# The last four down-projection tiles: one pair of tiles as seven products, placed between the other pair's two plain tiles

## The chip, the cores and the metric

The kernel runs on one core of one Trainium2 chip. The metric is the device time of one execution in microseconds; the median of three runs stands for a kernel. The profile is taken from one further execution. Engine names in the profile: PE is TensorE (matmul), PEld its weight load, DVE is VectorE, ACT is ScalarE, POOL is GpSimd, SP is SyncE, from which all transfers are issued here.

## The reference

```python
x = A_x                                          # 2048 tokens x 448
a, b = x_norm @ dft_hid_re.T, x_norm @ dft_hid_im.T
h  = x + dft_seq_re @ a - dft_seq_im @ b         # Fourier mixing
g, u = h_norm @ w_gate, h_norm @ w_up            # 448 -> 1792
h2 = h + (gelu(g) * u) @ w_down                  # 1792 -> 448, added to h
```

x_norm and h_norm are layer norms over the 448 columns. The change touches only the last line's product, `(gelu(g) * u) @ w_down`, called "down" here, for the last 512 of the 2048 tokens.

## The kernel before

**Products.** Every f32 operand is split into two f16 numbers, a high half (`hi_part`, line 103, on ACT) and a low half (`lo_part`, line 107 or 109, on DVE: the operand less its high half). A product of two operands is three f16 matmuls: high x high, high x low, low x high.

**Down in pairs.** The tokens are handled in pairs of tiles, p = 0 to 7, each of two 128-token tiles (g = 0, 1). The contraction of 1792 is cut into 14 slices f of 128; chunk n (0 to 6, `NC` = 7) joins slices n and n + 7. A pair's hidden values for one chunk are then a 2 x 2 matrix of blocks (g by slice), and the weights for the chunk are a 2 x 2 matrix of blocks too (slice by half of the 448 output columns, `HD` = 224). Pairs 0 to 5 multiply these 2 x 2 matrices with seven block products in place of eight: `strassen_mm` (line 651) runs 7 products x 3 terms = 21 matmuls of 128 x 224 per chunk, into four PSUM banks `a0` to `a3`. The list `STRASSEN` (line 147) names, in order, which of seven left operands meets which of seven right ones:

```python
STRASSEN = [(0, 5), (1, 4), (3, 0), (2, 1), (6, 6), (5, 3), (4, 2)]
```

Left operands 0 and 1 are blocks of the hidden values themselves; 2 to 6 are sums and differences of blocks. For pairs 0 to 5 these are made one or more chunks ahead by `dn_sums` (line 804: two POOL instructions of 256 elements a partition, one DVE add of 128) and split by `dn_split` (line 811). The right operands (`wd`, line 670) are made once, early. After its seventh chunk, a pair is drained (class `Drain`, line 603): ACT copies two banks to SBUF (`copy`), DVE adds three and then one half bank into the result `hr` (`bank2`, `bank3`, line 621), and POOL adds the copies in eight instructions (`sums`, line 649); `dn_store` (line 842) sends the 448 KB to DRAM.

**The last two pairs.** Pairs 6 and 7 hold the tokens of the last quarter (q = 3), whose hidden values come out while pairs 2 to 5 are multiplied. They are not summed: `last_hi` and `last_lo` (lines 854 and 857) split each slice f into `last["h"]` in f16 (both halves, all 14 slices, four tiles), as it is made. After the last gate/up step the four tiles (j, g), j = pair - 6, are multiplied plainly by `last_mm` (line 867): 14 slices x 3 terms x 2 column halves = 84 matmuls of 128 x 224 a tile. The diagonal weight blocks come from `wd`, the other two from `last["w"]`. `last_out` (line 886) adds a bank into `hr` on DVE and sends it off. The fourth tile is done in column halves, each with its own bank, so that only half of it is left to add and send at the end.

**What orders the work.** The scheduling is by hand: each engine runs its instructions in the order in which the code issues them, and waits in that order. A table `side` (line 904) holds pieces of side work by step t and place k; `do(t, k)` issues them. At the end of the loop over t, pair 5 is still being drained: `do(N_GU, k)` issues the last slices' high and low halves, pair 5's `bank3` and the first two of its eight POOL sums; `do(N_GU + 1, 3)` to `do(N_GU + 3, 3)` issue the other six and the store, in the code before right after the first plain tile. Buffers rotate: `hq`, `dn_s` have two each, `dn_w` three.

Of the kernel before, what the change touches and what calls it, by code (L numbers as in the profile page):

```python
# [8 lines left out]
F16 = mybir.dt.float16  # L9
F32 = mybir.dt.float32  # L10
# [3 lines left out]
P = 128  # L14
# [18 lines left out]
def kernel(  # L33
# [6 lines left out]
    w_down: bass.AP,  # L40
    out: bass.AP,
):

# [24 lines left out]
    V, A, G, PE = nc.vector, nc.scalar, nc.gpsimd, nc.tensor  # L70
# [7 lines left out]
    ps_tr = ctx.enter_context(tc.tile_pool(name="ps_tr", bufs=1, space=bass.MemoryType.PSUM))  # L78
# [23 lines left out]
    def hi_part(dst, src, scale=1.0):  # L102
        A.activation(dst, src, AF.Copy, scale=scale)  # L103

    def lo_part(dst, src, hi, scale=1.0):
        if isinstance(scale, float) and scale == 1.0:
            V.tensor_sub(dst, src, hi)  # L107
        else:
            V.scalar_tensor_tensor(dst, src, scale, hi, op0=ALU.mult, op1=ALU.subtract)  # L109
# [181 lines left out]
    class Weights:  # L291
# [8 lines left out]
        def sums(self):  # L300
            gate, up = self.raw[:, 0], self.raw[:, 1]
            s = self.s = dft.tile([P, 10, P], F32, tag="s", name=f"gu_s{self.f}")
            V.tensor_add(s[:, 0:3], up[:, 0:3], up[:, 3:6])
            V.tensor_sub(s[:, 3:6], s[:, 0:3], gate[:, 0:3])
            V.tensor_sub(s[:, 6:8], gate[:, 0:2], up[:, 0:2])
            V.tensor_sub(s[:, 8:10], gate[:, 4:6], s[:, 4:6])
# [194 lines left out]
    for k, f in enumerate(reversed(range(NF))):  # L501
        n = 17 + 3 * k
# [4 lines left out]
    for b in range(NB):  # L507
        for j in range(2):
            n = (b + 1) * NT + 1 + 6 * j
# [41 lines left out]
    for n in range(N_STEPS):  # L551
        b, c = divmod(n, NT)
# [50 lines left out]
    class Drain:  # L603
# [27 lines left out]
        def bank3(self):  # L631
            self.add(3, 6, 1.0)

        def sums(self, parts):
            x11, x12, x21, x22 = self.x
            M3, M4, M2, M5 = self.v
            ops = (
                (G.tensor_add, x12, M3),
                (G.tensor_sub, x21, M4),
                (G.tensor_add, x21, M2),  # L640
                (G.tensor_add, x12, M5),
                (G.tensor_sub, x11, M4),
                (G.tensor_add, x22, M3),
                (G.tensor_sub, x11, M5),
                (G.tensor_sub, x22, M2),
            )
            for k in parts:
                op, x, m = ops[k]
                op(x, x, m)

    def strassen_mm(acc, a_of, b_of, first, last, products):

        for n in products:
            k, m = divmod(n, 3)
            a, b = STRASSEN[k]
            la, lb = ((0, 0), (0, 1), (1, 0))[m]

            PE.matmul(  # L658
                acc[k // 2][:, k % 2 * HD : (k % 2 + 1) * HD],
                a_of(la, a),  # L660
                b_of(lb, b),
                start=first and m == 0 and k % 2 == 0,
                stop=last and m == 2,
                skip_group_check=True,
            )

    fpool = ctx.enter_context(tc.tile_pool(name="fpool", bufs=1, side="right", reuse_waits="tile"))
    ps_gu = ctx.enter_context(tc.tile_pool(name="ps_gu", bufs=1, space=bass.MemoryType.PSUM, reuse_waits="tile"))
    ps_dn = ctx.enter_context(tc.tile_pool(name="ps_dn", bufs=1, space=bass.MemoryType.PSUM, reuse_waits="tile"))
    wd = fpool.tile([P, NF // 2, 2, 7, HD], F16, name="wd")  # L670
# [29 lines left out]
    TQ = 2 * P  # L700
# [25 lines left out]
    def ftile(tag, bufs, name, n=TQ):  # L726
        return fpool.tile([P, n], F32, tag=tag, bufs=bufs, name=name)

    hh, hq = {}, {}
# [67 lines left out]
    NC = NF // 2  # L797
    dn_s, dn_w, acc_d, hr = {}, {}, {}, {}
# [5 lines left out]
    def dn_sums(d):  # L804
        t = dn_hid(d)
        s = dn_s[d] = fpool.tile([P, 5, P], F32, tag="dn_s", bufs=2, name=f"dn_s{d}")
        G.tensor_add(s[:, 0:2], t[:, 0:2], t[:, 2:4])  # L807
        G.tensor_sub(s[:, 2:4], t[:, 1:4:2], t[:, 0:4:2])
        V.tensor_add(s[:, 4], t[:, 0], t[:, 3])

    def dn_split(d):
        w = dn_w[d] = fpool.tile([P, 2, 7, P], F16, tag="dn_w", bufs=3, name=f"dn_w{d}")
        for src, dst in ((dn_hid(d)[:, 0:4:3], slice(0, 2)), (dn_s.pop(d), slice(2, 7))):
            hi_part(w[:, 0, dst], src)
            lo_part(w[:, 1, dst], src, w[:, 0, dst])
# [21 lines left out]
    def dn_drain(p):  # L837
        v = [ftile(f"v{k}", 1, f"v{k}_{p}", D) for k in range(2)]
        return Drain(hr[p], acc_d.pop(p), v, 1.0 / (H_SC * W_SC))

    def dn_store(p):
        nc.sync.dma_start(outr[p // 4, p % 4], hr[p])
# [3 lines left out]
    last = {}  # L846
# [20 lines left out]
    def last_mm(j, g, banks):  # L867

        tok = slice(g * TQ + j * P, g * TQ + (j + 1) * P)
        one = len(banks) == 1  # L870
        for cs in ((0, 1),) if one else ((0,), (1,)):
            for f in range(NF):
                k, n = divmod(f, NC)
                for m, (lh, lw) in enumerate(((0, 0), (0, 1), (1, 0))):
                    for c in cs:
                        w = wd[:, n, lw, k] if c == k else last["w"][:, lw, n, k]
                        PE.matmul(  # L877
                            banks[0][:, c * HD : (c + 1) * HD] if one else banks[c][:, 0:HD],
                            last["h"][:, lh, f, tok],
                            w,  # L880
                            start=f == 0 and m == 0 and c == cs[0],
                            stop=f == NF - 1 and m == 2,
                            skip_group_check=True,
                        )

    def last_out(j, g, ps, c, n):
        p = 6 + j
        h = hr[p][:, g, c * HD : (c + n) * HD]
        V.scalar_tensor_tensor(h, ps[:, 0 : n * HD], 1.0 / (H_SC * W_SC), h, op0=ALU.mult, op1=ALU.add)
        nc.sync.dma_start(outr[p // 4, p % 4][:, g, c * HD : (c + n) * HD], h)  # L890

    def dn_ahead(t):

        if t in (NF - 4, NF - 1):
            dn_sums(int(t == NF - 1))
        if t == NF - 2:
            dn_split(0)
        if NF <= t < 6 * NC + 12:
            dn_sums(t - 12)

    N_GU = 4 * NF
# [4 lines left out]
    def do(t, k):  # L906
        for what in side.pop((t, k), ()):
            what()
# [25 lines left out]
    for t in range(3 * NF, N_GU):  # L934
        f = t % NF
        if f < NF - 1:
            n, k = divmod(f, 2)
# [28 lines left out]
    for t in range(N_GU):  # L966
        q, f = divmod(t, NF)
# [24 lines left out]
        if q == 0:  # L992
            dn_ahead(t)
            cur.xy()
            prev = cur
            cur = GateUp(t + 1)
            cur.open()
            prev.yz()
            if d == -1:
                prev.c12_plus()  # L1000
            continue
# [3 lines left out]
        dn_mm(d, range(0, 8))  # L1005
        cur.xy()
        dn_ahead(t)
        dn_mm(d, range(8, 18))
        do(t, 1)
# [11 lines left out]
    prev.c_last()  # L1021
    for k in (1, 2, 0, 3):
        do(N_GU, k)
    banks = [(ps_tr, "tr"), (ps_gu, "X"), (ps_gu, "Y"), (ps_gu, "Z"), (ps_dn, "a0")]
    banks = [pool.tile([P, 512], F32, tag=tag, name=f"last_{tag}") for pool, tag in banks]
    for i in range(4):
        j, g = divmod(i, 2)
        last_mm(j, g, banks[i : i + 1] if i < 3 else banks[3:5])
        if i < 3:
            last_out(j, g, banks[i], 0, 2)  # L1030
        else:
            last_out(j, g, banks[3], 0, 1)
            last_out(j, g, banks[4], 1, 1)
        for t in range(N_GU + 1, N_GU + 4) if i == 0 else ():
            do(t, 3)
    assert not side


# [57 lines left out]
```

## Time and profile before

| what | us |
|---|---|
| median of 3 runs (728.07 to 730.27) | 728.22 |
| the profiled execution, its own time | 729.39 |
| its span, first to last instruction | 727.6 |
| TensorE busy | 719.5 |
| VectorE busy | 500.1 |
| ScalarE busy | 271.5 |
| GpSimd busy | 234.3 |
| the four plain tiles, first matmul to last tile's end | 692.1 to 724.5 |
| first plain tile starts / second / third | 692.1 / 700.2 / 708.2 |

The span is what the profile can see; the execution's time holds a further 1.8 us around it. A line of the profile names the source line, the engine, the instruction, the tiles written and read, its shape, and the count. In a timeline the first two numbers are the start and the duration in us, and a bracket gives the idle time before the instruction and what ended it. In a table of windows each engine has its busy time in the window and its count of instructions. In a group of instructions the numbers behind the bar are the busy time in us and the mean duration of one in ns.

### The profile page before, as it was taken

What the parts mean: (1) busy time and instruction counts of PE and PEld (TensorE: products, weight loads), DVE (VectorE), ACT (ScalarE), POOL (GpSimd) and SP (SyncE); (2) the same over time, 40 slices, a digit from 0 to 9 for tenths busy, and PEclk for the clock granted to TensorE, in tenths of its full rate; (3) what the DMA queues carried; (4) which work ended last, traced back from release to release, by engine and by line L of the source; (5) the groups of instructions that cost most, each with busy time, mean ns of one, the idle gap of its engine ahead of it and who ended that gap; (6) DMA issues with size and microseconds to landing.
All of it is one profiled execution on the core that took longest, in us unless ns stands there. A gap on an engine that the chain in (4) does not pass through costs nothing.

```text
span 727.6 us, 13421 instructions
## 1 busy us (share of the span) xinstructions
PE 719.5 (99%) x5330; PEld 499.2 (69%) x5330; DVE 500.1 (69%) x1026; ACT 271.5 (37%) x535; POOL 234.3 (32%) x274
## 2 busy tenths in 40 slices
PE   8999999999999999999999999999999999999998
PEld 5444444444444444444488889999999999999998
DVE  6888657486665866440477778788787877989730
ACT  4444704156133452221144443443444433454410
POOL 0000000000000001000057865577676766858430
PEclk9999999999999999999999999999999999999999
DMA  8766566577657976621057754757538496556411
GB/s 278 227 223 223 176 224 202 183 215 271 232 195 225 305 249 246 245 91 37 26 173 271 245 180 173 196 179 209 187 113 262 163 210 221 193 205 203 153 39 39
DMA packets 63518, 139.83 MB, mean 192 GB/s; under 512 B 30304, under 2 KB 39520, under 8 KB 63456
## 3 DMA queue, kind: packets, MB, share of 16 engines
q1 hardware_dynamic: 63456, 138.99, 58.0%
q8 instruction: 41, 0.67, 0.4%
q14 instruction: 21, 0.17, 0.1%
HBM read 112.23 MB, written 20.19 MB: 182 GB/s over the span
## 4 chain that ended last, share of the span: by engine, by line
PE 94%; DMA 3%; DVE 1%; ACT 1%; issue 0%; SPq 0%; DVEq 0%
PE acc L410 33%; PE pY L714 13%; PE acc_d L658 11%; PE y L475 9%; PE pX L714 9%; PE pZ L714 9%; PE acc L424 6%; DMA gw<-w_dram 2%; PE last_Y L877 1%; PE last_X L877 1%; PE last_tr L877 1%; DMA x<-in_x_dram 1%; PE last_a L877 1%; PE last_Z L877 1%; DMA wr<-in_w_seq_dram 1%; DVE ws L109 0%
## 5 line engine op out<-in xcount | busy, mean ns | idle before, releaser
L410 PE MATMUL acc<-ws,xs 128*128 128x512 f16 x1152 | 254.1, 379 | 0.9 <-ACT xs L103 0.6
L714 PEld LDWEIGHTS <-gw 128*128 128x128 f16 x2067 | 201.6, 98 | 24.9 <-DMA gw<-w_dram 2.1
L410 PEld LDWEIGHTS <-xs 128*128 128x128 f16 x1152 | 111.2, 98 | 139.6 <-issue 6.1
L714 PE MATMUL pY<-hops,gw 128*128 128x256 f16 x901 | 123.0, 273 | 1.6 <-DVE u L724 1.5
L658 PE MATMUL acc_d<-wd,dn_w 128*128 128x224 f16 x882 | 105.1, 259 | 0.0
L201 POOL TENSOR_TENSOR wd_s<-wd 128x448 f32<-128x448 f32 x7 | 7.9, 1131 | 274.1 <-DVE gu_w L109 274.1
L109 DVE SCALAR_TENSOR_TENSOR ws<-wr,ws 128x1024 f16<-128x1024 f32 (+1 forms) x66 | 77.9, 1187 | 15.2 <-ACT ws L103 15.2
L103 ACT ACTIVATE ws<-wr 128x1024 f16<-128x1024 f32 (+1 forms) x66 | 66.2, 1019 | 57.4 <-DMA wr<-in_w_seq_dram 28.0
L658 PEld LDWEIGHTS <-dn_w 128*128 128x128 f16 x882 | 85.1, 98 | 2.8
L714 PE MATMUL pX<-hops,gw 128*128 128x256 f16 x583 | 81.0, 273 | 1.0 <-DMA gw<-w_dram 0.9
L714 PE MATMUL pZ<-hops,gw 128*128 128x256 f16 x583 | 79.2, 273 | 0.0
L781 POOL TENSOR_TENSOR hh<-hh,g 128x256 f32<-128x256 f32 x42 | 31.0, 738 | 144.5 <-DVE hh L724 143.4
L724 DVE SCALAR_TENSOR_TENSOR u<-pY,u 128x256 f32<-128x256 f32 x112 | 46.9, 419 | 27.9 <-ACT c L788 19.0
L475 PE MATMUL y<-wh,z 128*128 128x448 f16 x336 | 65.7, 352 | 0.0
L483 DVE SCALAR_TENSOR_TENSOR hx<-y,hx 128x448 f32<-128x448 f32 x16 | 10.0, 625 | 78.1 <-PE y L475 78.1
L752 ACT ACTIVATE u<-pX 128x256 f32<-128x256 f32 x56 | 21.4, 383 | 90.9 <-PE pX L714 90.7
L475 PEld LDWEIGHTS <-z 128*128 128x128 f16 x336 | 32.8, 98 | 31.6 <-issue 0.4
L107 DVE TENSOR_TENSOR dn_w<-dn_s,dn_w 128x640 f16<-128x640 f32 x42 | 53.0, 1261 | 1.6 <-ACT dn_w L103 1.2
L765 ACT ACTIVATE g<-pX 128x256 f32<-128x256 f32 x56 | 21.4, 383 | 74.4 <-PE pX L714 69.1
L790 POOL TENSOR_TENSOR hh<-hh,c 128x256 f32<-128x256 f32 x42 | 40.8, 972 | 17.3 <-ACT c L788 17.1
L424 PE MATMUL acc<-ws,xs 128*64 128x512 f16 x384 | 44.7, 381 | 0.0
L807 POOL TENSOR_TENSOR dn_s<-hh 128x256 f32<-128x256 f32 x42 | 43.6, 1038 | 0.0
(107 smaller groups left out, 806.0 us busy)
## 6 DMA issues: line engine op xcount, KB each, us to landing
gw<-w_dram SPq DMA_DIRECT2D x53, 896.0 KB, 4.8
wr<-in_w_seq_dram SPq DMA_DIRECT2D x62, 512.0 KB, 5.9
w_dram<-gu_w SPq DMA_DIRECT2D x14, 896.0 KB, 4.7
gu_raw<-in_w_gu_dram SPq DMA_DIRECT2D x28, 384.0 KB, 5.8
wd<-in_w_down_dram SPq DMA_DIRECT2D x14, 448.0 KB, 5.4
x<-in_x_dram SPq DMA_DIRECT2D x16, 224.0 KB, 3.1
hx<-in_x_dram SPq DMA_DIRECT2D x8, 448.0 KB, 6.7
h_dram<-hx SPq DMA_DIRECT2D x8, 448.0 KB, 3.0
```

What stands on the lines that cost most here:

```text
L103: A.activation(dst, src, AF.Copy, scale=scale)
L107: V.tensor_sub(dst, src, hi)
L109: V.scalar_tensor_tensor(dst, src, scale, hi, op0=ALU.mult, op1=ALU.subtract)
L410: PE.matmul(acc[b, 3 * part + k], xs[c][:, lx, k * P : (k + 1) * P], seq_w(n, lw, part), start=c == 0 and m == 0, stop=c == NT - 1 and m == 2,
L424: PE.matmul(acc[b, 6][64 * part : 64 * part + 64, :], xs[c][:, lx, 3 * P :], seq_w(n, lw, part), start=c == 0 and m == 0, stop=c == NT - 1 ...
L475: PE.matmul(y[:, :D], z[b][:, lz, k, i * P : (i + 1) * P], wh[:, lw, k, :], start=k == 0 and m == 0, stop=k == 6 and m == 2,)
L658: PE.matmul(acc[k // 2][:, k % 2 * HD : (k % 2 + 1) * HD], a_of(la, a), b_of(lb, b), start=first and m == 0 and k % 2 == 0, stop=last and ...
L714: PE.matmul(ps, w[:, wl, wa + ws, :], ops[:, m + ms, :], start=first and n == 0, stop=last and n == len(terms) - 1, skip_group_check=True,)
L724: V.scalar_tensor_tensor(dst, ps, SC, other, op0=ALU.mult, op1=ALU.add)
L790: G.tensor_mul(c22, c22, self.c12)
L807: G.tensor_add(s[:, 0:2], t[:, 0:2], t[:, 2:4])
L877: PE.matmul(banks[0][:, c * HD : (c + 1) * HD] if one else banks[c][:, 0:HD], last["h"][:, lh, f, tok], w, start=f == 0 and m == 0 and c = ...
```

## The change

Pair 7's first tile, (1, 0), is now the first plain tile, and its second, (1, 1), the last one, in column halves. Between them pair 6 is multiplied in the seven-product form, 7 chunks of 21 matmuls, from the f16 halves in `last["h"]`. Its left operands 0 and 1 are read from `last["h"]` directly. For operands 2 to 6 new functions first rebuild the f32 values of the four blocks from their halves (`last_sums`: two DVE adds of 256 with f16 inputs and f32 output), then make the sums (a POOL add of 256, a DVE subtraction of 256, a DVE add of 128), and split them (`last_split`: ACT's high half and DVE's low half, 640 elements each). Sums are issued two chunks ahead, splits one chunk ahead; those of chunks 0 and 1 are issued ahead of the first plain tile and of six of pair 5's eight POOL sums. Pair 6 is drained like the others, except that its eight sums run on DVE instead of POOL, and it is stored in one transfer of 448 KB.

```diff
-        def sums(self, parts):
+        def sums(self, parts, E=G):
...
-                (G.tensor_add, x12, M3),
+                (E.tensor_add, x12, M3),
...
+    def last_sums(n):
+
+        h = last["h"].rearrange("p l f (g j t) -> p l f g j t", g=2, j=2)[:, :, :, :, 0]
+        v = fpool.tile([P, 4, P], F32, tag="hq", bufs=2, name=f"last_v{n}")
+        for k in range(2):
+            f = n + k * NC
+            V.tensor_add(v[:, 2 * k : 2 * k + 2], h[:, 0, f], h[:, 1, f])
+        s = fpool.tile([P, 5, P], F32, tag="dn_s", bufs=2, name=f"last_s{n}")
+        G.tensor_add(s[:, 0:2], v[:, 0:2], v[:, 2:4])
+        V.tensor_sub(s[:, 2:4], v[:, 1:4:2], v[:, 0:4:2])
+        V.tensor_add(s[:, 4], v[:, 0], v[:, 3])
+        last["s", n] = s
+
+    def last_split(n):
+        s = last.pop(("s", n))
+        w = last["a", n] = fpool.tile([P, 2, 7, P], F16, tag="dn_w", bufs=3, name=f"last_a{n}")
+        hi_part(w[:, 0, 2:7], s)
+        lo_part(w[:, 1, 2:7], s, w[:, 0, 2:7])
+
+    def last_pair_mm(n):
+        w = last.pop(("a", n))
+        h = last["h"]
+
+        def a_of(l, a):
+            return w[:, l, a] if a > 1 else h[:, l, n + a * NC, a * TQ : a * TQ + P]
+
+        strassen_mm(acc_d[6], a_of, lambda l, b: wd[:, n, l, b, :], n == 0, n == NC - 1, range(21))
...
-    banks = [(ps_tr, "tr"), (ps_gu, "X"), (ps_gu, "Y"), (ps_gu, "Z"), (ps_dn, "a0")]
+    banks = [(ps_tr, "tr"), (ps_gu, "X"), (ps_gu, "Y")]
     banks = [pool.tile([P, 512], F32, tag=tag, name=f"last_{tag}") for pool, tag in banks]
-    for i in range(4):
-        j, g = divmod(i, 2)
-        last_mm(j, g, banks[i : i + 1] if i < 3 else banks[3:5])
-        if i < 3:
-            last_out(j, g, banks[i], 0, 2)
-        else:
-            last_out(j, g, banks[3], 0, 1)
-            last_out(j, g, banks[4], 1, 1)
-        for t in range(N_GU + 1, N_GU + 4) if i == 0 else ():
-            do(t, 3)
+    last_sums(0)
+    last_sums(1)
+    last_split(0)
+    last_mm(1, 0, banks[:1])
+    for n in range(2):
+        do(N_GU + 1 + n, 3)
+    acc_d[6] = [ps_dn.tile([P, 512], F32, tag=f"a{k}", name=f"acc_d6_{k}") for k in range(4)]
+    for n in range(NC):
+        if n + 2 < NC:
+            last_sums(n + 2)
+        if n + 1 < NC:
+            last_split(n + 1)
+        last_pair_mm(n)
+        if n == 0:
+            do(N_GU + 3, 3)
+            last_out(1, 0, banks[0], 0, 2)
+    drain = dn_drain(6)
+    drain.copy()
+    drain.bank2()
+    drain.bank3()
+    drain.sums(range(8), V)
+    dn_store(6)
+    last_mm(1, 1, banks[1:])
+    last_out(1, 1, banks[1], 0, 1)
+    last_out(1, 1, banks[2], 1, 1)
```

More of the change, by code (lines that the diff above doesn't have):

```diff
@@ L637, in sums @@
             ops = (
-                (G.tensor_add, x12, M3),
[L639 to L645, printed above, removed]
+                (E.tensor_add, x12, M3),
+                (E.tensor_sub, x21, M4),
+                (E.tensor_add, x21, M2),
+                (E.tensor_add, x12, M5),
+                (E.tensor_sub, x11, M4),
+                (E.tensor_add, x22, M3),
+                (E.tensor_sub, x11, M5),
+                (E.tensor_sub, x22, M2),
             )
```

## The prediction, made before the result was known

> **What bounds the kernel now.** I read the page first (busy time by engine, then the chain that ended last), then that chain in order of time, then the last 36 us as a timeline and as a table of windows.
>
> ```profile
> span 727.6 us, 13421 instructions
> PE 719.5 (99%) x5330; PEld 499.2 (69%) x5330; DVE 500.1 (69%) x1026; ACT 271.5 (37%) x535; POOL 234.3 (32%) x274
> PE 94%; DMA 3%; DVE 1%; ACT 1%; issue 0%; SPq 0%; DVEq 0%
> ...
> 692.30 8.05 PE last_tr L877 x84
> 700.35 8.05 PE last_X L877 x84
> 708.40 8.05 PE last_Y L877 x84
> 716.45 4.03 PE last_Z L877 x42
> 720.48 4.04 PE last_a L877 x42
> ```
>
> TensorE sets the time: it holds 94% of the chain. Its last stretch is the four plain tiles of the change, 84 matmuls in 8.05 us each, so one 128x224 matmul every 8.05 / 84 = 0.0958 us. The windows show who has room there:
>
> ```profile
> core 0: us, PE busy (x) PEld busy (x) DVE busy (x) ACT busy (x) POOL busy (x), PEclk, DMA share, GB/s
> 692.10:700.10 8.00, 8.00 (x87) 8.00 (x85) 3.65 (x7) 1.25 (x3) 6.88 (x10) 1.00 0.01 2
> 700.10:708.20 8.10, 8.10 (x87) 8.10 (x85) 0.62 (x1) 0.00 (x0) 0.00 (x0) 1.00 0.23 85
> 708.20:716.20 8.00, 8.00 (x87) 8.00 (x85) 0.62 (x1) 0.00 (x0) 0.00 (x0) 1.00 0.09 31
> ```
>
> From 700 to 716 VectorE (DVE) works 0.62 us per tile, ScalarE (ACT) and GpSimd (POOL) not at all. That idleness is what the change spends. Whether it is enough is the question.
>
> **What goes.** Pair 6 takes 7 chunks x 21 products = 147 matmuls of the same 128x224 form in place of 2 x 84 = 168. That is 21 x 0.0958 = 2.01 us off TensorE, 0.28% of 728.22. This is the most that can be won; about 0.3% (2.2 us) is also what a measurement of this kernel can tell from no change.
>
> **What comes: operands that must be made in time.** Plain tiles read finished halves. Now each chunk needs two DVE adds of 256, a DVE subtraction of 256, a DVE add of 128 and a POOL add of 256, then ACT's high half and DVE's low half of 640. The first six products of a chunk (STRASSEN rows (0,5) and (1,4)) read h itself and wait for nothing new. The seventh waits for the high half, the ninth for the low half: a low half is due 8 x 0.0958 = 0.77 us after its chunk's start, and a chunk lasts 2.01 us on TensorE. DVE's prices:
>
> ```profile
> 305.79 0.55 DVE L303 TENSOR_TENSOR gu_s<-gu_raw 128x384 f32<-128x384 f32 x1
> 306.38 0.56 DVE L304 TENSOR_TENSOR gu_s<-gu_s,gu_raw 128x384 f32<-128x384 f32 x1
> 306.85 0.42 DVE L305 TENSOR_TENSOR gu_s<-gu_raw 128x256 f32<-128x256 f32 x1
> 307.19 0.42 DVE L306 TENSOR_TENSOR gu_s<-gu_raw,gu_s 128x256 f32<-128x256 f32 x1
> ...
> 646.59 0.28 DVE L809 TENSOR_TENSOR dn_s<-hh 128x128 f32<-128x128 f32 x1
> 646.79 0.38 DVE L109 SCALAR_TENSOR_TENSOR w_last<-wd,w_last 128x224 f16<-128x224 f32 x1
> ...
> 682.16 0.81 DVE L107 TENSOR_TENSOR dn_w<-dn_s,dn_w 128x640 f16<-128x640 f32 x1
> ```
>
> The first L305 runs 0.42 and the next instruction starts after 0.34: a queue advances by the duration less 0.08. So 256 costs 0.34, 128 costs 0.20 (646.59 to 646.79), 640 costs 0.73. L304 reads what L303 wrote and starts 0.59 after it instead of 0.47, so a dependent instruction pays 0.12 more; the subtraction is one. The sums of a chunk are 3 x 0.34 + 0.12 + 0.20 = 1.34, with the low half 0.73 it is **2.07 us of DVE per chunk, alone**. Already that is no less than TensorE's 2.01. The two adds read 16-bit inputs and write f32, a form the trace does not have. Bounds: the 128 row (0.20 step, half the elements) and the 256 row (0.34). I take 0.34, since every two-input row above goes by its element count whatever the types.
>
> **DVE is not alone.** The same low half beside POOL:
>
> ```profile
> 675.89 1.34 DVE L107 TENSOR_TENSOR dn_w<-dn_s,dn_w 128x640 f16<-128x640 f32 x1
> 677.16 0.41 DVE L724 SCALAR_TENSOR_TENSOR u<-pY,u 128x256 f32<-128x256 f32 x1
> ...
> 675.64 0.92 POOL L790 TENSOR_TENSOR hq<-hq,c 128x256 f32<-128x256 f32 x1
> 676.52 1.30 POOL L807 TENSOR_TENSOR dn_s<-hh 128x256 f32<-128x256 f32 x1
> 681.22 0.73 POOL L790 TENSOR_TENSOR hq<-hq,c 128x256 f32<-128x256 f32 x1 [0.95 <-ACT c L788]
> ```
>
> At 682.16 POOL has just finished (681.22 + 0.73 = 681.95) and the 640 takes 0.81. At 675.89 POOL is inside a 256 multiply, and the 640 takes 1.34; the POOL add behind it takes 1.30 in place of 0.73. They took turns: POOL's L790 first, then the whole 640, then L807. So each POOL instruction that meets waiting DVE work costs DVE 1.34 - 0.81 = **0.53 us**. L724, which reads one operand from PSUM, keeps its 0.41 to 0.42. The 16-bit adds beside POOL are again not in the trace; bounds 0 and 0.53 for these two of the five instructions. I take 0.53: the low half has one 16-bit input of its two and pays it.
>
> The Trainium skill, "SBUF — State Buffer", section "Who interferes with whom", says that a VectorE instruction with two SBUF inputs and a GpSimd instruction that reads SBUF exclude each other for the whole instruction, whatever the type; by it the adds collide too and the sum below stands, without it the first bound would hold. The same skill's "VectorE: DVE Perf Modes", section "Mode 2×_1P", wants every tensor 16-bit for two results a cycle, so by it the f32 output keeps the adds at 0.34.
>
> **The sum.** Where DVE and POOL stand as the tiles begin:
>
> ```profile
> 693.94 5.43 POOL L649 TENSOR_TENSOR hr<-hr,v 128x224 f32<-128x224 f32 x8
> 695.69 0.38 DVE L621 SCALAR_TENSOR_TENSOR hr<-acc_d,hr 128x224 f32<-128x224 f32 x1
> 700.19 0.26 PE L877 MATMUL last_X<-wd,h_last 128*128 128x224 f16 x1
> 700.39 0.62 DVE L889 SCALAR_TENSOR_TENSOR hr<-last_tr,hr 128x448 f32<-128x448 f32 x1 [4.32 <-PE last_tr L877]
> 708.24 0.26 PE L877 MATMUL last_Y<-wd,h_last 128*128 128x224 f16 x1
> ```
>
> The new sums stand in DVE's queue behind L621, so they start at 695.69 + 0.38 - 0.08 = 695.99. POOL runs two of pair 5's eight L649 first, then the adds of chunks 0 and 1, then four L649, chunk 2's add, two more L649, then one add per chunk. So the L649, which now run beside an idle DVE after 696, move into DVE's busy time.
>
> - Low half 0: 2 x 1.34 + 0.73 and three POOL turns (two adds, one L649) 1.59: 700.99, its end 701.07. Due at 700.19 + 0.77 = 700.96: TensorE loses some 0.1.
> - Low half 1: sums of chunk 2 and the low half, 2.07, and five DVE instructions that each find POOL ahead (L649 and chunk 2's add), 2.65: 705.71. TensorE, due about 703.0, idles some 2.6 us.
> - The out pass of tile (1,0), 0.62 - 0.08 = 0.54, stands behind it: 706.25.
> - Low halves 2 to 5: 2.07 + 0.53 = 2.60 each: 716.65, end 716.73. Low half 6 needs no more sums and is early.
> - TensorE then needs 0.04 to start, a weight load (98 ns, row below) and 13 + 21 products, 3.26 us: 716.73 + 3.40 = 720.13.
>
> ```profile
> L658 PEld LDWEIGHTS <-dn_w 128*128 128x128 f16 x882 | 85.1, 98 | 2.8
> 675.08 0.73 ACT L103 ACTIVATE dn_w<-dn_s 128x640 f16<-128x640 f32 x1
> ```
>
> Before, the fourth tile starts at 708.24 + 8.05 = 716.29. So the last tile starts **3.84 us later**, where 2.01 earlier was possible. ACT's 0.73 per chunk is hidden beside DVE. What waits behind the ninth product is all of TensorE's queue; behind a low half on DVE, the next sums; on SP, pair 5's store waits for the last L649 (about 705) and only out transfers stand behind it, for which nobody waits.
>
> **The end.** The last tile has 8.05 us on TensorE, its first half 4.03. In that time DVE drains pair 6: four adds from PSUM and eight sums of 224. POOL is then idle.
>
> ```profile
> L621 DVE SCALAR_TENSOR_TENSOR hr<-acc_d,hr 128x224 f32<-128x224 f32 x24 | 8.7, 383 | 0.2
> L617 ACT ACTIVATE v<-acc_d 128x448 f32<-128x448 f32 x12 | 5.8, 537 | 0.0
> out_dram<-hr SPq DMA_DIRECT2D x6, 448.0 KB, 3.0
> 724.54 0.39 DVE L889 SCALAR_TENSOR_TENSOR hr<-last_a,hr 128x224 f32<-128x224 f32 x1 [3.63 <-PE last_a L877]
> 724.96 0.33 SPq L890 DMA_DIRECT2D out_dram<-hr  x1
> ```
>
> 4 x 0.30 + 2 x 0.12 + 8 x 0.34 = 4.2 us at the 256 price: the first half's out pass may be 0.2 late, the final one, at 8.05, is not. Had the sums the contended price of 0.34 + 0.53, it were 8.4, a loss of 0.35; without POOL work I take 0. Pair 6's store leaves at about 4.5 and needs 3.0, done before the final transfer at 8.5. From TensorE's end to the span's end stay 3.1 us (724.5 to 727.6).
>
> The profiled execution took 729.39 us with its span of 727.6, 1.17 above the median 728.22. The sum is a difference within it: span 731.4, run 733.2, and on the median 728.22 + 3.8 = **732.0 us**.
>
> **Rivals.**
> - *DVE keeps up* (not slower). If POOL costs DVE nothing, DVE needs 7 x 2.07 + 0.54 = 15.03 from 695.99, 711.0, and low half 6 is due at 700.19 + 12.06 + 0.77 = 713.0: no lasting stall, 728.22 - 2.0 = 726.2. The place is the turn-taking; it comes out even where a POOL turn costs about half of 0.53. For it: DVE's idle windows and its head start of 4 us. Against it: the 1.34 rows. 8%.
> - *The 16-bit adds are cheap.* At the 128 price, 0.28 less per chunk over seven chunks of sums is 1.96 less: +1.9, 730.1. If they only escape POOL's turns, most of the chunks' own turn falls on the other three instructions and only two of chunk 2's five vanish, about 1.0 less: 731.0. 17%.
> - *The clock falls.* The longest idle of TensorE on other engines in the trace is the row below, with the granted clock at 1.00; my 2.6 us is longer. At half clock a chunk takes 4.02: two such chunks from 706.9 put the last tile's start 1.0 later (733.0), four 4.9 later (736.9). The Trainium skill, "TensorE: Matmul & The Clock Gate", Part 1, halves the clock after an idle window of about 3.4 us; by that 2.6 is not enough, hence only 5%.
>
> ```profile
> PE pY L714 <- DVE u L724: 1.5, 1, 1.5
> ```
>
> **How the numbers follow.** Forecast 66% (731.0 to 733.2), cheap adds 17%, DVE keeps up 8%, clock 5%, something between (POOL turns half hidden, 0 to +2) 4%. The range is 729.0 to 734.0: it takes in the forecast, the cheap adds and the milder clock case and leaves out about 15%. Slower by over 0.3% (above 730.4): the forecast, the clock and two thirds of the cheap adds, 82%. Within: the rest of these, the middle, and most of the 726.2 case, which at -0.28% is inside the bound: 15%. Faster: 3%.
>
> **What would show it.** In the profile after: low halves of 640 at 1.3 us and not 0.8; POOL adds at 1.3; TensorE waiting on DVE from about 703 to 705.7 and then some 0.6 in each of four chunks; DVE near full from 696 to 717. Wrong, if TensorE shows no such waits, if the f16 adds last 0.28, or if the last tile starts before 716.3.

## The result, and the profile after

| | before | changed |
|---|---|---|
| median us (6 runs each) | 728.82 (728.07 to 730.27) | 732.49 (731.51 to 734.36) |
| ratio to before | | 1.0049 (95% interval 1.0031 to 1.0067) |
| span of the profiled execution | 727.6 | 730.1 |
| first plain tile's first matmul | 692.14 | 691.25 |
| last tile's first matmul | 716.29 | 718.68 |
| **D**, the time between these two | 24.15 | 27.43 |
| last tile's first matmul to the end of the span | 11.3 | 11.4 |

The change made the kernel slower, by 3.7 us between the medians. The stages in front vary by up to two microseconds from one profiled execution to the next, also where the code in front is the same (the first plain tile starts between 690.37 and 692.32 us); in that of the changed kernel they were 0.89 us shorter than before. So D, which leaves them out, is what the experiments below compare: it rose by 3.28 us to 27.43. The 231 products in it, 84 of the first tile and 147 of the pair, would take 231 x 0.0958 = 22.13 without a wait.

TensorE of the changed kernel, as a timeline; the bracket is the idle time before the group and what ended it:

```profile
691.25 0.26 PE L879 MATMUL last_tr<-wd,h_last 128*128 128x224 f16 x1
...
699.30 0.74 PE L660 MATMUL acc_d<-wd,h_last 128*128 128x224 f16 x6
699.88 1.70 PE L660 MATMUL acc_d<-wd,last_a 128*128 128x224 f16 x15
...
704.49 1.42 PE L660 MATMUL acc_d<-wd,last_a 128*128 128x224 f16 x13 [2.14 <-DVE last_a L109]
...
707.62 1.42 PE L660 MATMUL acc_d<-wd,last_a 128*128 128x224 f16 x13 [0.94 <-DVE last_a L109]
710.21 1.42 PE L660 MATMUL acc_d<-wd,last_a 128*128 128x224 f16 x13 [0.41 <-DVE last_a L109]
712.81 1.42 PE L660 MATMUL acc_d<-wd,last_a 128*128 128x224 f16 x13 [0.41 <-DVE last_a L109]
715.41 1.42 PE L660 MATMUL acc_d<-wd,last_a 128*128 128x224 f16 x13 [0.41 <-DVE last_a L109]
718.68 0.74 PE L879 MATMUL last_X<-wd,h_last 128*128 128x224 f16 x6
```

Each group of 13 is a chunk from its ninth product on, and from chunk 1 to chunk 5 each waits for a low half (L109) from VectorE. Chunk 0 loses only 0.1 (its group of 15 lasts 1.70, that of the last chunk 1.60), chunk 1 waits 2.14 us, and the last three groups start 2.60 us apart, against 2.01 of matmuls in a chunk. The waits add up to 4.3 us:

```profile
PE acc_d L660 <- DVE last_a L109: 4.3, 5, 2.1
```

D is 5.30 above 22.13 all the same. A row's wait begins at the end of the last product, 0.26 after its start, while products that do not wait start 0.0958 apart; so each of the five waits costs TensorE some 0.17 more than its row says, and chunk 0 adds its 0.1.

VectorE and GpSimd at low half 0, chunk 2's sums and low half 1 (to 704.4), and in a late chunk:

```profile
698.83 1.27 DVE L109 TENSOR_TENSOR last_a<-last_s,last_a 128x640 f16<-128x640 f32 x1
700.03 1.68 DVE L900 TENSOR_TENSOR last_v<-h_last 128x256 f32<-128x256 f16 x2
701.74 0.77 DVE L903 TENSOR_TENSOR last_s<-last_v 128x256 f32<-128x256 f32 x1
702.43 0.81 DVE L904 TENSOR_TENSOR last_s<-last_v 128x128 f32<-128x128 f32 x1
703.16 1.28 DVE L109 TENSOR_TENSOR last_a<-last_s,last_a 128x640 f16<-128x640 f32 x1
704.36 0.61 DVE L891 SCALAR_TENSOR_TENSOR hr<-last_tr,hr 128x448 f32<-128x448 f32 x1
...
707.48 0.75 DVE L900 TENSOR_TENSOR last_v<-h_last 128x256 f32<-128x256 f16 x2
708.26 0.42 DVE L903 TENSOR_TENSOR last_s<-last_v 128x256 f32<-128x256 f32 x1
708.61 0.81 DVE L904 TENSOR_TENSOR last_s<-last_v 128x128 f32<-128x128 f32 x1
709.34 0.81 DVE L109 TENSOR_TENSOR last_a<-last_s,last_a 128x640 f16<-128x640 f32 x1
710.08 0.75 DVE L900 TENSOR_TENSOR last_v<-h_last 128x256 f32<-128x256 f16 x2
```

```profile
698.72 3.50 POOL L651 TENSOR_TENSOR hr<-hr,v 128x224 f32<-128x224 f32 x4
702.18 0.90 POOL L902 TENSOR_TENSOR last_s<-last_v 128x256 f32<-128x256 f32 x1
703.05 1.90 POOL L651 TENSOR_TENSOR hr<-hr,v 128x224 f32<-128x224 f32 x2
...
708.37 0.90 POOL L902 TENSOR_TENSOR last_s<-last_v 128x256 f32<-128x256 f32 x1 [1.70 <-DVE last_v L900]
```

The same instructions, two prices. While GpSimd works through pair 5's sums (L651), the two adds take 1.68 and the low half 1.28. In the late chunk, where GpSimd has one add (708.37 to 709.27), the adds take 0.75 and the low half 0.81, and one instruction pays: the 128 add, 0.81, which before took 0.28 alone. VectorE has no gap in either: 707.48 to 710.08 is one period of 2.60. The out pass (L891), which reads one operand from PSUM, keeps its 0.61 beside GpSimd.

### The profile page after: what moved, and what is told of

Same layout as the page of the kernel before. It is cut to its first block, busy times and chain, and to the rows that moved or that the text cites. A ratio compares the mean times of both kernels' runs of the same rounds, so it can differ in the third digit from the quotient of the medians.

```text
span 730.1 us, 13452 instructions
## 1 busy us (share of the span) xinstructions
PE 718.5 (98%) x5309; PEld 497.9 (68%) x5309; DVE 523.0 (72%) x1071; ACT 277.9 (38%) x544; POOL 242.1 (33%) x281
## 4 chain that ended last, share of the span: by engine, by line
PE 93%; DVE 4%; DMA 1%; ACT 1%; issue 1%; POOL 0%; POOLq 0%; DVEq 0%; ACTq 0%
PE acc L412 34%; PE pY L716 13%; PE acc_d L660 12%; PE y L477 9%; PE pZ L716 9%; PE pX L716 9%; PE acc L426 6%; DMA gw<-w_dram 1%; PE pw L99 1%; DVE last_v L900 1%; DVE last_a L109 1%; DVE last_s L904 1%; PE last_Y L879 1%; PE last_X L879 1%; DVE last_s L903 0%
## 5 line engine op out<-in xcount | busy, mean ns | idle before, releaser
L109 DVE TENSOR_TENSOR dn_w<-dn_s,dn_w 128x640 f16<-128x640 f32 x42 | 53.0, 1261 | 1.6 <-ACT dn_w L105 1.2
```

## The experiments

**Theory:** VectorE feeds the pair, and each GpSimd instruction with SBUF operands that meets two-input work on VectorE costs it a turn of about 0.5 us. **Rivals:** VectorE's own instructions are the bound and GpSimd costs nothing; the seven-product form is slower on TensorE by itself; the pair's drain lies on the path.

### 1. Without six of pair 5's sums

```diff
-    for n in range(2):
-        do(N_GU + 1 + n, 3)
+    for n in range(3):
+        kept = side.pop((N_GU + 1 + n, 3))
+        for what in kept[1:]:
+            what()
...
-            do(N_GU + 3, 3)
```

> Leaves out: six of the eight sums that GpSimd adds into pair 5's result; everything else is the changed kernel. Measure D: from the first matmul of the first plain tile to the first matmul of the last tile; 24.15 us before, 27.43 in the changed kernel, 22.13 if no product waited (231 x 0.0958). Theory (VectorE and GpSimd take turns, and TensorE waits for VectorE): the turns ahead of low half 1 go from about four to two and the 2.1 us wait shrinks to some 0.3; from low half 2 on the period stays 2.60 us. D 24.8 to 25.3. Rival (VectorE's own instructions are too many, GpSimd costs nothing): D stays 27.4.

D was 25.23. VectorE around low half 1, and TensorE at chunk 1 and at the first wait that the profile lists, in chunk 2:

```profile
698.95 0.74 DVE L900 TENSOR_TENSOR last_v<-h_last 128x256 f32<-128x256 f16 x2
699.73 0.43 DVE L903 TENSOR_TENSOR last_s<-last_v 128x256 f32<-128x256 f32 x1
700.08 0.81 DVE L904 TENSOR_TENSOR last_s<-last_v 128x128 f32<-128x128 f32 x1
700.81 0.81 DVE L109 TENSOR_TENSOR last_a<-last_s,last_a 128x640 f16<-128x640 f32 x1
```

```profile
701.28 1.82 PE L660 MATMUL acc_d<-wd,last_a 128*128 128x224 f16 x15
...
704.81 1.42 PE L660 MATMUL acc_d<-wd,last_a 128*128 128x224 f16 x13 [0.94 <-DVE last_a L109]
```

With GpSimd otherwise idle, chunk 2's sums and low half 1 take 2.67 us in place of 4.41 (700.03 to 704.44 in the changed kernel), and of the 2.14 wait some 0.22 is left (chunk 1's group of 15 lasts 1.82 in place of 1.60). Not one VectorE instruction was removed. The rival that GpSimd costs nothing falls. From chunk 2 on the period is still 2.60.

### 2. The chunk's add on VectorE; 3. the same, and without the six sums

```diff
-        G.tensor_add(s[:, 0:2], v[:, 0:2], v[:, 2:4])
+        V.tensor_add(s[:, 0:2], v[:, 0:2], v[:, 2:4])
```

Experiment 3 has the edits of 1 and 2.

> The one GpSimd add of each chunk runs on VectorE instead (0.34 us more there per chunk, one instruction more). D is 27.43 in the changed kernel. Theory (turns of 0.53): the period of the late chunks falls from 2.60 to 2.07 + 0.34 = 2.41, VectorE meets only the six sums of pair 5, D 26.0 to 26.5. Rival (VectorE's own instruction time bounds): the period rises by 0.34 and D by some 2 us, to 29.4.

> Leaves out: six of the eight sums into pair 5's result; and the GpSimd add of each chunk runs on VectorE, so that GpSimd is idle beside the whole of the pair's preparation. Theory (turns): every two-input VectorE instruction takes its time alone (640: 0.81, 256: 0.41, 128: 0.28), period 2.41, D 23.4 to 24.1. Rival (instruction time): D 29.4, as when only the add is moved.

D was 26.23 in experiment 2 and 23.87 in experiment 3. A chunk of experiment 3, with GpSimd idle:

```profile
704.41 0.75 DVE L900 TENSOR_TENSOR last_v<-h_last 128x256 f32<-128x256 f16 x2
705.20 0.42 DVE L902 TENSOR_TENSOR last_s<-last_v 128x256 f32<-128x256 f32 x1
705.54 0.42 DVE L903 TENSOR_TENSOR last_s<-last_v 128x256 f32<-128x256 f32 x1
705.87 0.28 DVE L904 TENSOR_TENSOR last_s<-last_v 128x128 f32<-128x128 f32 x1
706.08 0.82 DVE L109 TENSOR_TENSOR last_a<-last_s,last_a 128x640 f16<-128x640 f32 x1
706.81 0.76 DVE L900 TENSOR_TENSOR last_v<-h_last 128x256 f32<-128x256 f16 x2
```

Giving VectorE one instruction more (0.34) made the chunk shorter, 706.81 - 704.41 = 2.40 against 2.60. These are the prices of the instructions alone: the two 16-bit adds 0.75 together, so no cheaper than f32 ones. But with every turn gone D is only 0.28 below before: 2.40 a chunk is still more than TensorE's 2.01. The turns explain the loss against before; VectorE's own work, the moved add in it, takes most of the gain. What the pair would do with VectorE at 2.06 a chunk and no turns, no run shows.

### 4. All operands ready

```diff
-        w = last.pop(("a", n))
+        w = last["a", 0]
...
-    last_sums(1)
...
-        if n + 2 < NC:
-            last_sums(n + 2)
-        if n + 1 < NC:
-            last_split(n + 1)
```

Every chunk reads chunk 0's left operands 2 to 6; operands 0 and 1 still come from its own slices.

> Leaves out: the sums and splits of chunks 1 to 6; all seven chunks multiply chunk 0's left operands, which are ready before the pair starts. It measures what the seven-product form is worth on TensorE with no wait, and the drain behind it. Theory: D 22.1 to 22.3, that is 1.9 to 2.0 less than before, and the time from the last tile's first matmul to the end of the span stays 11.3 to 11.4 as in both kernels. Rival (the form itself is slower on TensorE, by switching banks or operands): D above 22.8 without a wait on another engine.

D was 22.13 and no product waited; the span ended 11.4 after the last tile's first matmul. So the form is worth 24.15 - 22.13 = 2.02 us on TensorE, and it is all lost, and more, to waiting.

### 5. The drain's sums on GpSimd

```diff
-    drain.sums(range(8), V)
+    drain.sums(range(8))
```

> One part undone: the eight sums of pair 6's drain run on GpSimd, as for pairs 0 to 5, instead of VectorE. Prediction's step on the end: whatever they cost lies beside the last tile's 8.05 us. GpSimd needs 8 x 0.68 = 5.4 us in place of VectorE's 2.7, so pair 6's store leaves at about 6.9 us after the last tile's first matmul instead of 4.2, and lands at about 10.3, where the last transfer starts at 8.7. D stays 27.4 within 0.4; the time from the last tile's first matmul to the end of the span goes from 11.4 to 11.4 to 11.8. Rival (the drain sits on the path): 2.7 later, 14.1.

D was 27.43 and the rest 11.4, both as in the changed kernel; only the size of the delay was off:

```profile
718.38 5.09 POOL L651 TENSOR_TENSOR hr<-hr,v 128x224 f32<-128x224 f32 x8 [3.60 <-ACT v L619]
...
723.50 0.38 SPq L844 DMA_DIRECT2D out_dram<-hr  x1
```

GpSimd starts as soon as the first copied bank is there, before the last tile begins (719.00), and the store leaves 4.5 us after that, not 6.9. The drain is off the path on either engine.

### 6. The six sums behind chunk 6's add

```diff
-    for n in range(2):
-        do(N_GU + 1 + n, 3)
...
-            do(N_GU + 3, 3)
...
+        if n == 4:
+            for k in range(3):
+                do(N_GU + 1 + k, 3)
```

> Nothing is left out: the six sums of pair 5 are issued on GpSimd behind chunk 6's add, instead of in front of chunk 2's. Theory (turns, and it matters where they fall): low half 1 is early as without the six sums (D 25.23 there); the six now meet at most low halves 5 and 6 and cost one turn on low half 5. D 25.2 to 25.8, some 1.3 above before. Rival (the six sums cost the same wherever they stand): D 27.4.

D was 25.70, in the range: the waits are 0.94, 0.41, 0.41 and, where low half 5 now meets these sums, 0.88. Of the 2.2 us that leaving the sums out had saved, moving them saves 1.7. So it is their place that costs.

### 7. An early start

```diff
-        v = fpool.tile([P, 4, P], F32, tag="hq", bufs=2, name=f"last_v{n}")
+        v = ring.tile([P, 4, P], F32, tag="w", bufs=3, name=f"last_v{n}")
...
+    at(side, (N_GU - 1, 0), lambda: last_sums(0))
+    at(side, (N_GU - 1, 1), lambda: last_split(0), lambda: last_sums(1))
...
-    last_sums(0)
-    last_sums(1)
-    last_split(0)
```

> Nothing is left out: the sums of chunk 0 stand at the start of the last gate/up step, its split and the sums of chunk 1 in the middle of it, where VectorE idles about 3 us; the buffers for the rebuilt values come from the ring of gate/up weights, which is free by then. The rest is the changed kernel, the six sums of pair 5 included. Theory (VectorE is short of time, not of speed at one point): all low halves come 2.5 to 3.1 earlier, D 24.3 to 25.0, and the gate/up step in front is no longer. Rival (a wait on the sums of pair 5 or a buffer holds the chunks back): D above 26.5.

D was 25.87: better by 1.56, but neither what was expected nor the rival. Chunk 2's sums started 698.42 - 691.42 = 7.00 us after the first plain tile, in the changed kernel 700.03 - 691.25 = 8.78, so the head start was 1.78 and not 2.5 to 3.1. I had counted idle time that lies in pieces:

```profile
691.37 0.82 DVE L109 TENSOR_TENSOR last_a<-last_s,last_a 128x640 f16<-128x640 f32 x1 [0.45 <-ACT last_a L105]
692.11 0.75 DVE L900 TENSOR_TENSOR last_v<-h_last 128x256 f32<-128x256 f16 x2
```

Low half 0 itself waits 0.45 for ScalarE, and chunk 1's sums stand behind it and ahead of the last gate/up results. The gate/up step in front was no longer than before (6.27 us from its first product to the first plain tile in both).

### 8. Early start, little GpSimd; 9. early start, no GpSimd

Both have the edits of 7 and move the out pass of tile (1, 0) behind low half 6. In the first, each add but chunk 6's is on VectorE and pair 5's six sums stand on GpSimd behind chunk 6's:

```diff
-        G.tensor_add(s[:, 0:2], v[:, 0:2], v[:, 2:4])
+        (G if n == NC - 1 else V).tensor_add(s[:, 0:2], v[:, 0:2], v[:, 2:4])
...
-    for n in range(2):
-        do(N_GU + 1 + n, 3)
...
-        if n == 0:
-            do(N_GU + 3, 3)
+        if n == 4:
+            for k in range(3):
+                do(N_GU + 1 + k, 3)
+        if n == 5:
             last_out(1, 0, banks[0], 0, 2)
```

In the second all adds are on VectorE, and in place of the last part:

```diff
-        if n == 0:
-            do(N_GU + 3, 3)
+        if n == 5:
+            for k in range(3):
+                side.pop((N_GU + 1 + k, 3))
+            drains[5].sums(range(2, 8), V)
+            dn_store(5)
             last_out(1, 0, banks[0], 0, 2)
```

> Nothing is left out: early start as above; each chunk's add on VectorE but the last chunk's, which stays on GpSimd with the six sums of pair 5 behind it; the out pass of tile (1,0) behind low half 6. VectorE then needs 2.41 per chunk alone from about 3 us earlier and low half 5 is ready before TensorE asks for it. Theory: no wait of TensorE, D 22.1 to 22.5, the span 1.7 to 2.0 shorter than before on equal fronts, ratio to before 0.9972 to 0.9977 (726.2 to 726.8 for 728.2). Rival (the gate/up step in front pays for the earlier sums): D as said but the step longer by as much, ratio 1.000.

> Nothing is left out: as the last one (early start, out pass of tile (1,0) late), but all adds on VectorE and the six sums of pair 5 on VectorE too, behind low half 6, so that GpSimd does nothing beside the pair. In the last one the single wait, 0.56 us, came when low half 5 met chunk 6's GpSimd add and a sum of pair 5. Theory (turns): that wait goes, D 22.1 to 22.4, 1.8 to 2.0 below before, on equal fronts 0.9973 to 0.9975 of its time; the timed ratio 0.996 to 0.999, since the stages in front vary by as much between runs. Rival (VectorE alone is still too slow at 2.41 a chunk against 2.01): a wait of 0.5 or more on low half 5, D 22.6 to 23.0.

The first gave D 22.87, above its range, and a ratio to before of 0.9991 (0.9983 to 1.0000). By its D, 1.28 us less than before, 0.9982 was due, just outside the interval; its time is not told apart from no change. The gate/up step in front did not pay for the earlier sums: it took 6.27 us in both experiments, as before. The one wait of the first, and what VectorE and GpSimd did ahead of it:

```profile
710.72 1.42 PE L660 MATMUL acc_d<-wd,last_a 128*128 128x224 f16 x13 [0.56 <-DVE last_a L109]
```

```profile
709.38 2.48 DVE L109 TENSOR_TENSOR last_a<-last_s,last_a 128x640 f16<-128x640 f32 x2
```

```profile
709.27 4.96 POOL L651 TENSOR_TENSOR hr<-hr,v 128x224 f32<-128x224 f32 x6
```

Two low halves took 2.48 beside pair 5's sums. In the second these sums are behind them on VectorE, the two take 1.79, and the profile lists no wait of TensorE for a low half: D 22.21, and **0.9969 of the time before (0.9958 to 0.9981)**, 726.86 us against 729.06 in the same rounds. It is faster than before, and so than the changed kernel, which was slower than before. Its windows over the pair:

```profile
700.10:708.20 8.10, 8.10 (x88) 8.10 (x86) 8.00 (x21) 2.54 (x4) 0.00 (x0) 1.00 0.00 1
708.20:716.20 8.00, 8.00 (x85) 7.84 (x83) 7.68 (x21) 2.23 (x4) 0.00 (x0) 1.00 0.20 76
```

The columns are those of the table of windows in the prediction: TensorE is full, VectorE 7.7 to 8.0 of 8, GpSimd at zero. VectorE still needs 2.40 a chunk, so what carries the pair is its lead, which shrinks from chunk to chunk: low half 1 ended at 701.28 and was due at 702.06 + 0.77 = 702.83, low half 5 ended at 710.89 and was due at 710.11 + 0.77 = 710.88. With a chunk more TensorE would have waited, by these figures.

### 10. The cost doubled

```diff
+        G.tensor_add(s[:, 0:2], v[:, 0:2], v[:, 2:4])
         G.tensor_add(s[:, 0:2], v[:, 0:2], v[:, 2:4])
```

> The suspected cost doubled: the GpSimd add of each chunk is done twice, the same values to the same place; VectorE's instructions are those of the changed kernel. Theory (each GpSimd instruction that finds VectorE at two-input work costs it 0.53): the period of the late chunks goes from 2.60 to 3.1, D from 27.43 to 29.5 to 31.0. Rival (GpSimd's time is hidden, VectorE's instruction count bounds): period 2.60 and D 27.4 to 28.0.

D was 30.62. TensorE's late groups:

```profile
712.55 1.42 PE L660 MATMUL acc_d<-wd,last_a 128*128 128x224 f16 x13 [0.94 <-DVE last_a L109]
715.68 1.42 PE L660 MATMUL acc_d<-wd,last_a 128*128 128x224 f16 x13 [0.94 <-DVE last_a L109]
718.80 1.42 PE L660 MATMUL acc_d<-wd,last_a 128*128 128x224 f16 x13 [0.94 <-DVE last_a L109]
```

The period is 3.13 in place of 2.60: one GpSimd add of 256 more per chunk costs TensorE 0.53 us, the price that the prediction took from 1.34 - 0.81. An add of 128 (0.28 to 0.81) and a low half of 640 (0.81 to 1.34, in the kernel before) lose the same 0.53. So the loss goes by GpSimd's instruction and not by VectorE's, as turns would have it and a common slowing of both would not.

## Why the prediction came out

**What is won.** 21 matmuls, 2.01 us: experiment 4 measured 2.02. Right.

**VectorE's 2.07 per chunk, the 16-bit adds at 0.34.** Experiment 3's period of 2.40 is 2.06 and the moved add's 0.34. Right, and the rival of the cheap adds falls with it. The Trainium skill, "VectorE: DVE Perf Modes", section "What auto-detection actually checks", has VectorE pack two 16-bit values only if every tensor is 16-bit. The trace agrees: with an f32 output the two adds took 0.75.

**Turns of 0.53, for the 16-bit adds too.** Shown by taking GpSimd's instructions away (1 to 3) and by adding one (10). The two adds took 1.68 beside GpSimd and 0.75 alone. The Trainium skill, "SBUF — State Buffer", section "Who interferes with whom", says that a VectorE instruction with two SBUF inputs contends with a GpSimd instruction that reads SBUF, and the trace agrees. The rival that VectorE keeps up fails on its condition that GpSimd costs VectorE nothing: experiment 1 took GpSimd's six sums away and D fell by 2.20. Its other half, that VectorE at 2.07 a chunk would be in time, was not run; in experiment 3, at 2.40, TensorE waits in four chunks.

**The sum.** Low half 0 was due to end at 701.07 and ended at 700.10, which on the front of before is 700.99. The period of 2.60 is exact. The term that was mis-sized is low half 1: "five DVE instructions that each find POOL ahead", 2.65. Against their times alone the five lost 2.28: the adds 0.93, the subtraction 0.35, the 128 add 0.53, the low half 0.47. The 0.53 had been taken beside a GpSimd instruction of 256 elements, and only the 128 add met one here. The others met sums of 224. Alone, GpSimd did two of those in 1.28 ahead of the pair, 0.64 each, where one of 256 took 0.73. Experiment 2 has only sums of 224 beside chunk 0:

```profile
695.63 0.77 DVE L902 TENSOR_TENSOR last_s<-last_v 128x256 f32<-128x256 f32 x1
696.32 0.88 DVE L903 TENSOR_TENSOR last_s<-last_v 128x256 f32<-128x256 f32 x1
697.12 0.74 DVE L904 TENSOR_TENSOR last_s<-last_v 128x128 f32<-128x128 f32 x1
...
692.17 6.21 POOL L651 TENSOR_TENSOR hr<-hr,v 128x224 f32<-128x224 f32 x8
```

Against 0.42, 0.42 and 0.28 alone they lost 0.35, 0.46 and 0.46. So a turn behind a sum of 224 costs about 0.46, and the prediction priced it as one of 256. The instruction that reads what the two adds wrote loses less, 0.35 in both kernels. It starts some 0.12 later, and may find the sum already under way and wait only for its rest; no run tests that by itself. Low half 1 ended at 705.33 on the front of before, not 705.79. That 0.46 is most of the difference between the 3.84 forecast and the 3.28 of D. Between the medians it is 3.67, so the 732.0 forecast and the 732.49 measured agree better than the sum deserves.

**Which instruction pays.** "Low halves of 640 at 1.3 us" was wrong for the late chunks: they ran in 0.81, and the 128 add in front of them took the turn. "POOL adds at 1.3" was wrong too: they took 0.90. The sum did not depend on either.

**The end.** 11.3 before, 11.4 after, 11.4 with the sums on GpSimd: nothing lost, as forecast.

**The clock.** It stayed at 1.00 through the wait of 2.14 us in the profiled execution. The rival did not happen there; the last section shows where it did.

## What to carry to other kernels

Fewer matmuls help only as long as the engine that prepares their operands takes less time per chunk than TensorE then needs, or has a lead that lasts to the end: work out that engine's period alone, and again with what its neighbour does. VectorE instructions with two SBUF operands and GpSimd instructions took turns here, so an add moved from busy VectorE to idle GpSimd cost 0.53 us where VectorE would have done it in 0.34. Old work on GpSimd, which before had stood beside an idle VectorE, cost 2.2 us once VectorE was the bound; where it stands in the order is part of the change.

## What was not expected of the hardware

In experiment 10 the granted clock fell behind an idle of 2.14 us. In the profiled executions of the changed kernel and of experiment 5 the idle was as long, and the clock stayed at 1.00. The third number from the end of a row is the clock:

```profile
704.00:705.00 1.00, 0.04 (x1) 0.05 (x2) 1.00 (x2) 0.00 (x0) 1.00 (x2) 1.00 0.00 0
705.00:706.00 1.00, 1.00 (x7) 0.80 (x8) 1.00 (x3) 0.00 (x0) 0.92 (x2) 0.53 0.00 0
706.00:707.00 1.00, 1.00 (x7) 0.80 (x6) 0.97 (x2) 0.62 (x1) 1.00 (x2) 0.50 0.00 0
707.00:708.00 1.00, 1.00 (x7) 0.80 (x6) 1.00 (x2) 0.12 (x1) 1.00 (x3) 0.50 0.00 0
708.00:709.00 1.00, 0.80 (x6) 0.43 (x3) 1.00 (x2) 0.00 (x0) 0.92 (x2) 0.76 0.10 38
```

By these rows TensorE had half its clock for some 3.4 us (0.94 of the second row, all of the next two, 0.48 of the last), and 13 matmuls took 2.54 us in place of 1.42. It cost little, since the next low half was later still. The Trainium skill, "TensorE: Matmul & The Clock Gate", Part 1, gives an idle window of about 3.4 us for this fall; here the clock fell once behind 2.14, and twice it did not. What else decides it, these runs do not show. Two of the six runs of the changed kernel had a mean clock of 0.997, and none of the thirty runs of the kernel before beside experiments 8 and 9 was under 0.999; that it fell at the same wait was not traced. One of these two was the fastest of the six, the other the slowest, so no price can be given.
